# Second product of three batches by seven half-size products instead of one full one

## The chip, the cores and the metric

The kernel runs on one core of a Trainium2 chip. TensorE (PE) multiplies matrices, with its weight loads on a row of their own (PEld); VectorE (DVE), ScalarE (ACT) and GpSimd (POOL) do elementwise work; SyncE (SP) issues most of the transfers. Each engine takes its instructions strictly in the order of the program, and engines wait for one another by semaphores. The metric is the time of one execution in microseconds: the kernel before takes 219.86 us as the median of three runs (219.19 to 220.28).

## The reference

Four batches of 768 rows and 8 heads go through a sparse attention, then through a two-layer network whose hidden width is 2048. Cut to what matters here:

```
# attention, per batch and head: a window of |i-j| < 16 on the keys,
# and 24 block keys (maximum over 32 rows) with 24 block means of v
a = softmax([mask(scale * q @ k.T), scale * q @ k_max.T + log 32])
x = a @ [v, v_mean]                      # 3072 x 512 over all batches
h = x @ w_in                             # first product, 3072 x 2048
g = h * sigmoid(beta * h)
out = g @ w_out                          # second product, 3072 x 512, float32
```

## The kernel before, in words

The work of a batch is attention (scores, exponential, mask, values, normalisation), a transposition of its result into `xT`, the first product into `h_sb` (16 tiles of 128 hidden columns by 768 rows, bf16), and the second product (6 tiles of 128 rows by 512 columns, each a sum over the 16 tiles of `h_sb`).

The order of the instructions is written by hand. `run(main, sides)` (L499) emits the steps of a list `main` one after the other, and after step i every side job whose position lies below i + 1. The main steps keep PE busy, and the side jobs do the attention of the next batch. In the loop over batches 1 to 3 a batch has two stages, which are called the first and the second stage of the batch here:

- First stage: 16 steps `h_tile` (L459), each 8 matmuls of 384 columns into one of three two-bank PSUM tiles `big`, then one ACT pass (Silu) into `h_sb`. Its side jobs prepare the next batch: POOL casts the keys to bf16 (`kq_cast`, L429), SP issues their transposition into `kT` (`kq_dma`, L434), DVE copies the key windows into `kw` and takes block maxima `km` (`windows_nat`, `key_max_nat`), POOL spreads the maxima (`key_sums`), then casts the queries and the values (`kq_cast`, `v_cast`). `v_odd_dma` copies shifted values from `ve` to `vo`.
- Second stage: 24 steps `o_atom` (L482), each 4 matmuls of 512 columns (`o_mm`, L472) into one of two one-bank PSUM tiles `one`. After each sixth of the rows `o_out` (L477) copies the bank to SBUF on DVE and SP issues the output. Its side jobs are the attention of the next batch for four pairs of heads g: `scores` (24 small matmuls into two `big` tiles), the exponential on ACT, the mask on DVE (`mask_e`), the block means (`vm_all`, then `spread` on DVE), the values product `av_at` into a `big` tile, the normalisation on DVE (`norm`: a reciprocal and a multiplication, the result called `xn`), and the transposition of `xn` into `xT`, which is issued from ACT's queue (`x_dma`, L422).

Batch 0 runs by a path of its own, whose second stage also uses `o_atom`, with the attention of batch 1 as side jobs. Batch 3 has no following batch, so its two stages have no side jobs. Its last 128 rows are computed as two halves of 256 columns, so that the last copy and the last output are short.

`natp` and `stage` are pools for casted and loaded keys and queries; a tile of a pool is written again when its last reader is done.

Of the kernel before, what the change touches and what calls it, by code (L numbers as in the profile page):

```python
# [11 lines left out]
def kernel(  # L12
# [10 lines left out]
    nc = tc.nc  # L23
# [48 lines left out]
    stg = {}  # L72
    loads = {}

    krow = const.tile([P, H // 2 * 16 * D], bf16, name="krow")
    qrow = const.tile([P, H // 2 * 16 * D], bf16, name="qrow")
    def row_view(t, b, lo, hi):
        c = CS[b]
        r = S // c
# [107 lines left out]
    h_sb = const.tile([P, k2, S], bf16, name="h_sb")  # L187
    w_in_sb = const.tile([P, k1, d_ff], bf16, name="w_in_sb")
    w_out_sb = const.tile([P, k2, d_model], bf16, name="w_out_sb")
    beta_sb = const.tile([P, k2], f32, name="beta_sb")  # L190
    inv_beta = const.tile([P, k2], f32, name="inv_beta")
    dummy = const.tile([P, 1], f32, name="dummy")
# [234 lines left out]
    nat = {}  # L427

    def kq_cast(eng, nm, b, g):  # L429
        t = natp.tile([P, J6, 2, D], bf16, name=nm + "n", tag=nm + "n")  # L430
        nat[(nm, b, g)] = t
        eng.tensor_copy(out=t[:], in_=stg[(nm, b, g)].rearrange("p h j d -> p j h d"))  # L432

# [16 lines left out]
        nc.scalar.activation(out=h_sb[:, i, lo:lo + HS], in_=t[:, 0:HS], func=ACTF.Silu, scale=beta_sb[:, i:i + 1])  # L450

    def h_part(i, k_lo, k_hi):
        t = big[i % 3]
        for kk in range(2):
            for ki in range(k_lo, k_hi):
                nc.tensor.matmul(t[:, kk, 0:HS], w_in_sb[:, ki, i * P:(i + 1) * P],  # L456
                                 xT[:, ki, kk * HS:(kk + 1) * HS], start=(ki == 0), stop=(ki == k1 - 1))

    def h_tile(i):  # L459
        t = big[i % 3]  # L460
# [16 lines left out]
    def o_out(b, ms, t):  # L477
        o = op.tile([P, d_model], f32, name="o_sb", tag="o_sb")
        (act_cp if b == 0 and ms < 3 else dve_cp)(o[:], t)
        nc.sync.dma_start(out=out_r[b * J6 + ms], in_=o[:])  # L480

    def o_atom(b, ms, a):  # L482
        t = one[ms % 2][:, 0]
        for n in range(4 * a, 4 * a + 4):
            o_mm(ms, n, t)
        if a == 3:
            o_out(b, ms, t)

    def warm(n, t):
        for _ in range(n):  # L490
# [186 lines left out]
    for g in range(G):  # L677
        s.append(((11.2, 14.35, 14.4, 14.5)[g], lambda g=g: x_dma(1, g)))
    s.append((6.5, lambda: load_keys(2)))
    run(main, s)  # L680


    for b in range(1, B):
        n = b + 1
        s = []
        if n < B:
            for g in range(2):
                s.append((0 + .1 * g, lambda g=g, n=n: hw_load("q", q, n, g)))
# [15 lines left out]
        run([lambda i=i: h_tile(i) for i in range(k2)], [x for x in s if x[0] < 16])  # L704
        s = [((x[0] - 16) * 1.2, x[1]) for x in late]
        if n < B:
            scores_at(n, s, [1, 5.9, 8, 10.1])
            av_at(n, s, [10.2, 13.1, 13.2, 13.3], [0, 1, 2, 0])
            for g in range(G):
                s.append(((10.3, 13.35, 13.4, 13.5)[g], lambda g=g: x_dma(n, g)))  # L710
            s.append((5.99, lambda: vm_all(big[0], VMC)))
            s.append((6.3, lambda: spread(0)))
            s.append((8.3, lambda: spread(1)))
            if n + 1 < B:
                s.append((7, lambda n=n: load_keys(n + 1)))
        main = [lambda ms=ms, a=a: o_atom(b, ms, a) for ms in range(J6 - (n == B)) for a in range(4)]
        run(main, s)
        if n == B:
            ms = J6 - 1
            for lo, hi in ((0, 256), (256, 512)):  # L720
                t = one[0 if lo else 1][:, 0]
                for kk in range(k2):
                    o_mm(ms, kk, t, lo, hi)
                o = op.tile([P, hi - lo], f32, name="o_half", tag=f"o_half{lo}", bufs=1)
                nc.vector.tensor_copy(out=o[:], in_=t[:, 0:hi - lo])
                nc.sync.dma_start(out=out_r[b * J6 + ms][:, lo:hi], in_=o[:])

# [1 line left out]
_INS = ['q', 'k', 'v', 'moe_w_in', 'moe_w_out', 'moe_beta']  # L729
# [26 lines left out]
```

## Time and profile before

| | |
|---|---|
| Median of three runs | 219.86 us |
| Span of the profiled execution | 217.3 us, 2.6 us under the median of the runs |
| PE busy | 207.7 us, 96% of the span |
| ACT, DVE, POOL busy | 108.7, 98.7, 55.8 us |
| Granted TensorE clock | full in every slice |

A span runs from the first to the last instruction of the profiled execution; what the runs take beyond it lies around the program. In a row of the timeline stand the start in us, the length in us, engine, line, operation, what is written from what, sizes and count, and in brackets the idle time before and who ended it. A row with a count merges instructions that follow each other. In the groups by line the number after the bar is the busy time in us, then the mean of one instruction in ns.

### The profile page before, as it was taken

The page shows a single profiled execution, that of the slowest core. Times are in us where ns is not written, and L with a number is a line of the kernel's source. Part 1 is how long each engine was busy: PE and PEld are TensorE (multiplying, and loading weights), DVE is VectorE, ACT ScalarE, POOL GpSimd, SP SyncE. Part 2 cuts the span into 40 slices and gives each one's busy share as a digit, 9 for nine tenths or more (in the row PEclk, how much of TensorE's full clock was granted, in tenths as well). Part 3 has the DMA queues.
Part 4 walks back from the last instruction along what each step waited for, and adds up shares of the span by engine and source line. Part 5 has one row for each costly group of instructions (what it writes and reads, how often), then busy time and mean ns, then how long its engine had stood idle before and what let it go on. Part 6 is the DMA issues. An engine that isn't in the chain of part 4 may idle for free.

```text
span 217.3 us, 5298 instructions
## 1 busy us (share of the span) xinstructions
PE 207.7 (96%) x2219; PEld 120.6 (56%) x2219; DVE 98.7 (45%) x232; ACT 108.7 (50%) x144; POOL 55.8 (26%) x89
## 2 busy tenths in 40 slices
PE   7669999999999999999999999999999999999993
PEld 6558766655445455655455456564555556554452
DVE  5378584797476720440589312521797200002121
ACT  2356776787767007666663037767570077750000
POOL 7708991011515600138203300247000000000000
PEclk9999999999999999999999999999999999999999
DMA  6995999999949979999769999999437410001212
GB/s 118 183 217 114 186 180 197 207 207 218 215 100 215 229 220 187 234 202 209 118 183 210 222 250 231 194 191 183 111 111 172 118 51 0 0 0 51 97 48 97
DMA packets 85271, 34.09 MB, mean 157 GB/s; under 512 B 73712, under 2 KB 82304, under 8 KB 85248
## 3 DMA queue, kind: packets, MB, share of 16 engines
q1 hardware_dynamic: 68192, 24.05, 54.4%
q0 software_dynamic: 7424, 7.34, 21.4%
q10 hardware_dynamic: 9632, 2.37, 6.6%
q8 instruction: 17, 0.28, 0.6%
q14 instruction: 6, 0.05, 0.1%
HBM read 27.37 MB, written 6.29 MB: 155 GB/s over the span
## 4 chain that ended last, share of the span: by engine, by line
PE 71%; DMA 14%; DVE 4%; POOL 3%; issue 3%; ACT 2%; SPq 0%; POOLq 0%; ACTq 0%
PE big L456 29%; PE one L474 28%; DMA vst<-in_v_dram 5%; PE big L442 5%; PE one L448 3%; DMA xT<-xn 3%; DMA w_in_sb<-in_moe_w_in_dram 3%; DMA krow<-in_k_dram 3%; PE big L448 2%; PE big L306 1%; POOL ve L324 1%; POOL e L319 1%; PE big L384 1%; DVE e L319 1%; ACT e L315 1%
## 5 line engine op out<-in xcount | busy, mean ns | idle before, releaser
L474 PE MATMUL one<-w_out_sb,h_sb 128*128 128x512 bf16 (+1 forms) x400 | 86.7, 371 | 0.0
L469 ACT ACTIVATE h_sb<-big,beta_sb 128x768 bf16<-128x768 f32 x48 | 42.7, 900 | 52.3 <-PE big L456 52.3
L456 PE MATMUL big<-xT,w_in_sb 128*128 128x384 bf16 x384 | 63.0, 326 | 0.1
L474 PEld LDWEIGHTS <-h_sb 128*128 128x128 bf16 x400 | 37.7, 98 | 40.5 <-issue 0.2
L456 PEld LDWEIGHTS <-w_in_sb 128*128 128x128 bf16 x384 | 37.6, 98 | 25.4 <-issue 0.3
L244 DVE COPY o_sb<-one 128x512 f32<-128x512 f32 x20 | 13.8, 688 | 48.1 <-PE one L474 44.9
L315 ACT ACTIVATE e<-big,bias 128x768 bf16<-128x768 f32 x32 | 27.4, 898 | 8.9 <-PE big L306 4.9
L319 DVE TENSOR_TENSOR e<-e,mask 128x768 bf16<-128x768 bf16 x22 | 13.6, 638 | 20.3 <-ACT e L315 19.4
L238 POOL COPY kw<-km 128x288 bf16<-128x288 bf16 x12 | 5.2, 436 | 50.6 <-DVE km L234 21.0
L324 POOL CAST ve<-vst 128x832 bf16<-128x832 f32 (+1 forms) x15 | 12.9, 875 | 14.1 <-DMA vst<-in_v_dram 12.5
L244 DVE COPY kw<-kT 128x1152 bf16<-128x1152 bf16 x8 | 3.8, 477 | 23.5 <-DMA kT<-kn 23.5
L234 DVE TENSOR_REDUCE km<-kT 128x24 bf16<-128x768 bf16 x12 | 11.2, 944 | 2.6 <-ACT kT L241 2.6
L411 DVE TENSOR_TENSOR xn<-big,r 128x768 bf16<-128x768 f32 x12 | 11.5, 957 | 0.4
L442 PE MATMUL big<-xT,w_in_sb 128*128 128x384 bf16 x64 | 11.4, 327 | 0.1
L432 POOL CAST kn<-kst 128x768 bf16<-128x768 f32 x8 | 6.5, 824 | 15.6 <-DMA kst<-in_k_dram 15.6
L583 ACT ACTIVATE h_sb<-big,beta_sb 128x384 bf16<-128x384 f32 x16 | 8.2, 581 | 3.7 <-PE big L442 3.7
L448 PEld LDWEIGHTS <-w_in_sb 128*128 128x128 bf16 x64 | 6.1, 98 | 4.0
L448 PE MATMUL one<-xT,w_in_sb 128*128 128x384 bf16 x44 | 8.1, 326 | 0.0
L306 PEld LDWEIGHTS <-kw 64*128 64x128 bf16 x288 | 4.9, 95 | 5.5 <-issue 4.2
L442 PEld LDWEIGHTS <-w_in_sb 128*128 128x128 bf16 x64 | 5.8, 98 | 3.7 <-DMA w_in_sb<-in_moe_w_in_dram 0.2
L384 PEld LDWEIGHTS <-e 128*64 128x64 bf16 x336 | 6.1, 111 | 2.3 <-issue 1.9
L450 ACT ACTIVATE h_sb<-one,beta_sb 128x384 bf16<-128x384 f32 x11 | 6.4, 580 | 1.2 <-PE one L448 0.6
(115 smaller groups left out, 191.3 us busy)
## 6 DMA issues: line engine op xcount, KB each, us to landing
out_dram<-o_sb SPq DMA_DIRECT2D x23, 256.0 KB, 2.4
vst<-in_v_dram SPq DMA_DIRECT2D x13, 336.0 KB, 4.6
kst<-in_k_dram SPq DMA_DIRECT2D x8, 384.0 KB, 6.7
qst<-in_q_dram SPq DMA_DIRECT2D x8, 384.0 KB, 4.2
w_in_sb<-in_moe_w_in_dram POOLq DMA_DIRECT2D x4, 512.0 KB, 7.5
w_out_sb<-in_moe_w_out_dram POOLq DMA_DIRECT2D x4, 512.0 KB, 13.7
vo<-ve SPq DMA_DIRECT2D x12, 107.2 KB, 2.3
vst<-in_v_dram SPq DMA_DIRECT2D x3, 416.0 KB, 8.2
```

What stands on the lines that cost most here:

```text
L234: nc.vector.tensor_reduce(out=km[g][:, NK:NK + nb], in_=kT[g][:, W:W + S].rearrange("p (n f) -> p n f", f=block), op=ALU.max, axis=AX.X)
L244: nc.vector.tensor_copy(out=o, in_=i)
L315: nc.scalar.activation(out=e[:], in_=s[:, :, 0:HS], func=ACTF.Exp, bias=bias[:, 0:1], scale=scale)
L319: (nc.gpsimd if (b, g) == (1, G - 1) else nc.vector).tensor_mul(out=e.rearrange("p h (m q) -> p h m q", q=QT), in0=e.rearrange("p h (m q) ...
L324: eng.tensor_copy(out=ve[:, g, lo:hi, 0:D], in_=vst[g][:, lo:hi])
L384: nc.tensor.matmul(tv[par * QT:(par + 1) * QT, j, h], e[:, h, lo:lo + QT], (vo if par else ve)[:, g, h * J6 + J, 0:D + 1], start=True, sto ...
L411: nc.vector.tensor_mul(out=x[:, 3 * us[0]:3 * us[0] + 3 * n].rearrange("p (k j) h d -> p k (j h) d", k=n), in0=tv[:, :, :, 0:D], in1=r[:, ...
L442: nc.tensor.matmul(t[:, 0:HS], w_in_sb[:, ki, i * P:(i + 1) * P], xT[:, ki, 0:HS], start=(ki == 0), stop=(ki == k1 - 1))
L448: nc.tensor.matmul(t[:, 0:HS], w_in_sb[:, ki, i * P:(i + 1) * P], xT[:, ki, lo:lo + HS], start=(ki == 0), stop=(ki == k1 - 1))
L456: nc.tensor.matmul(t[:, kk, 0:HS], w_in_sb[:, ki, i * P:(i + 1) * P], xT[:, ki, kk * HS:(kk + 1) * HS], start=(ki == 0), stop=(ki == k1 - 1))
L469: nc.scalar.activation(out=h_sb[:, i, :].rearrange("p (k m) -> p k m", k=2), in_=t[:, :, 0:HS], func=ACTF.Silu, scale=beta_sb[:, i:i + 1])
L474: nc.tensor.matmul(t[:, 0:hi - lo], h_sb[:, n, ms * P:(ms + 1) * P], w_out_sb[:, n, lo:hi], start=(n == 0), stop=(n == k2 - 1))
```

## The change

The second product of batches 1 to 3 is computed by a Strassen scheme (Winograd's form) on halves. `h_sb` is split in even and odd hidden tiles and in two halves of the rows (A11, A12, A21, A22), `w_out_sb` in even and odd hidden tiles and in two halves of the columns (B11 to B22). Seven products of half size in each direction replace eight. For one 128-row tile of a half (t = 0, 1, 2) a product is 8 matmuls of 256 columns, and it yields 128 rows of the upper and 128 rows of the lower half of the batch.

- `h_sums` forms S1, S2, S4 and S3 in bf16 on DVE, in five pieces per batch among the steps of the first stage (two hidden pairs, two, two, one, one). S3 overwrites A21 in `h_sb`.
- `w_sums` and `w_sums_late` form T1, T2, T4 and T3 once, at the end of batch 0's second stage and after the first step of batch 1's first stage.
- Products 1 and 2, 6 and 7, 5 and 3 share a PSUM bank and add up in it; product 4 has one to itself. The four banks are the two `one` tiles and the two banks of the first `big` tile.
- `gather` takes a partial result out of PSUM after each product: ACT copies after 1, 5 and 2, DVE adds after 6, 7 (two) and 3, POOL adds once after 7. It issues an output of 128 rows after 7 and after 3.
- The attention of the next batch loses the first `big` tile: `av_at` alternates between the other two, `vm_all` still goes to the first. The positions of the side jobs in the second stage are new, counted in 23 steps.
- To make room in SBUF the row-major keys and queries of the first batches share the space of the sums, and pools of keys and queries have fewer buffers. The fourth keys of a batch are loaded at the end of the second stage, into the buffer of the first.

```diff
-    natp = ctx.enter_context(tc.tile_pool(name="nat", bufs=4))
+    half = ctx.enter_context(tc.tile_pool(name="half", bufs=1))
+    natp = ctx.enter_context(tc.tile_pool(name="nat", bufs=2))
...
-        f = stage.tile([P, 2, J6, D], f32, name=nm + "st", tag=nm + "st")
+        f = stage.tile([P, 2, J6, D], f32, name=nm + "st", tag=nm + "st", bufs=3 if nm == "k" else 4)
...
-        t = natp.tile([P, J6, 2, D], bf16, name=nm + "n", tag=nm + "n")
+        t = natp.tile([P, J6, 2, D], bf16, name=nm + "n", tag=nm + "n", bufs=3 if nm == "k" else 2)
...
-        t = big[i % 3]
+        t = big[(i + 2) % 3]
...
+    S1, S2, S4, S3 = s_sb[:, 0], s_sb[:, 1], s_sb[:, 2], A21
+    T1, T2, T4, T3 = t_sb[:, 0], t_sb[:, 1], t_sb[:, 2], B12
+    OPERANDS = {1: (A11, B11), 2: (A12, B21), 3: (S4, B22), 4: (A22, T4), 5: (S1, T1), 6: (S2, T2), 7: (S3, T3)}
+    SLOTS = {1: one[0][:, 0, 0:DH], 6: one[1][:, 0, 0:DH], 4: big[0][:, 0, 0:DH], 5: big[0][:, 1, 0:DH]}
+    SLOTS[2], SLOTS[7], SLOTS[3] = SLOTS[1], SLOTS[6], SLOTS[5]
...
+    def h_sums(lo, hi):
+        j = slice(lo, hi)
+        tt(nc.vector, S1[:, j], A21[:, j], A22[:, j], ALU.add)
+        tt(nc.vector, S2[:, j], S1[:, j], A11[:, j], ALU.subtract)
+        tt(nc.vector, S4[:, j], A12[:, j], S2[:, j], ALU.subtract)
+        tt(nc.vector, S3[:, j], A11[:, j], A21[:, j], ALU.subtract)
...
+    def product(n, t, lo=0, hi=J2):
+        a, b = OPERANDS[n]
+        for j in range(lo, hi):
+            nc.tensor.matmul(SLOTS[n], a[:, j, t * P:(t + 1) * P], b[:, j],
+                             start=(j == 0 and n not in (2, 3, 7)), stop=(j == J2 - 1), skip_group_check=True)
...
+        if n in (1, 5):
+            part[n] = half.tile([P, DH], f32, name=f"p{n}", tag=f"p{n}")
+            act_cp(part[n][:], src)
+        elif n == 6:
+            tt(nc.vector, part[6][:], src, part[1][:], ALU.add)
+        elif n == 2:
+            act_cp(part["lo"][:, 0:DH], src)
+        elif n == 7:
+            tt(nc.vector, u3[:], src, part[1][:], ALU.add)
+            tt(nc.gpsimd, o[:, DH:], part[5][:], u3[:], ALU.add)
+            tt(nc.vector, o[:, 0:DH], SLOTS[4], u3[:], ALU.add)
+        elif n == 3:
+            tt(nc.vector, o[:, DH:], src, part[6][:], ALU.add)
...
+        def first():
+            product(4, 0, 0, J2 - 1)
+        def then():
+            product(1, 0, 0, J2 - 1)
+            product(4, 0, J2 - 1)
+            product(1, 0, J2 - 1)
+            gather(1, b, 0)
+        main = [first, then]
+        for t in range(J6 // 2):
+            for n in ((6, 5, 2, 7, 3) if t == 0 else (1, 6, 5, 4, 2, 7, 3)):
+                main.append(lambda n=n, t=t: step(n, t))
...
-        for g in range(G):
+        for g in range(G - 1):
             hw_load("k", k, n, g)
...
+        for at, lo, hi in ((4.9, 0, 2), (8.9, 2, 4), (12.4, 4, 6), (14.4, 6, 7), (15.9, 7, 8)):
+            s.append((at, lambda lo=lo, hi=hi: h_sums(lo, hi)))
+        run([lambda i=i: h_tile(i) for i in range(k2)], s)
+        s = [(x[0] - 16, x[1]) for x in late]
         if n < B:
-            scores_at(n, s, [1, 5.9, 8, 10.1])
-            av_at(n, s, [10.2, 13.1, 13.2, 13.3], [0, 1, 2, 0])
+            s.append((.05, exp_table))
+            scores_at(n, s, [1, 4.05, 6.05, 8.05])
+            av_at(n, s, [10.1, 11.1, 12.6, 13.7], [1, 2, 1, 2])
             for g in range(G):
-                s.append(((10.3, 13.35, 13.4, 13.5)[g], lambda g=g: x_dma(n, g)))
+                s.append(((10.3, 11.3, 12.8, 13.9)[g], lambda g=g: x_dma(n, g)))
...
+                s.append((20.5, lambda n=n: hw_load("k", k, n + 1, G - 1)))
+        run(second_product(b), s)
```

More of the change, by code (lines that the diff above doesn't have):

```diff
@@ L73 @@
     loads = {}
-    krow = const.tile([P, H // 2 * 16 * D], bf16, name="krow")
-    qrow = const.tile([P, H // 2 * 16 * D], bf16, name="qrow")
+    J2 = d_ff // P // 2
+    DH = d_model // 2
+    s_sb = const.tile([P, 3, J2, HS], bf16, name="s_sb")
+    rows = s_sb.rearrange("p a j s -> p (a j s)")
+    RW = H // 2 * 16 * D
+    krow, qrow = rows[:, 0:RW], rows[:, RW:2 * RW]
     def row_view(t, b, lo, hi):
@@ L189 @@
     w_out_sb = const.tile([P, k2, d_model], bf16, name="w_out_sb")
+    t_sb = const.tile([P, 3, J2, DH], bf16, name="t_sb")
     beta_sb = const.tile([P, k2], f32, name="beta_sb")
@@ L459, in h_tile @@
     def h_tile(i):
-        t = big[i % 3]
+        t = big[(i + 2) % 3]
         if i > 1:
@@ L487, in o_atom @@
             o_out(b, ms, t)
+    hv = h_sb.rearrange("p (j e) s -> p j e s", e=2)
+    wv = w_out_sb.rearrange("p (j e) d -> p j e d", e=2)
+    A11, A12, A21, A22 = [hv[:, :, e, u * HS:(u + 1) * HS] for u in range(2) for e in range(2)]
+    B11, B12, B21, B22 = [wv[:, :, e, u * DH:(u + 1) * DH] for e in range(2) for u in range(2)]
+    S1, S2, S4, S3 = s_sb[:, 0], s_sb[:, 1], s_sb[:, 2], A21
+    T1, T2, T4, T3 = t_sb[:, 0], t_sb[:, 1], t_sb[:, 2], B12
+    OPERANDS = {1: (A11, B11), 2: (A12, B21), 3: (S4, B22), 4: (A22, T4), 5: (S1, T1), 6: (S2, T2), 7: (S3, T3)}
@@ new lines, in w_sums, with w_sums_late @@
+    def w_sums():
+        tt(nc.vector, T1, B12, B11, ALU.subtract)
+        tt(nc.vector, T2, B22, T1, ALU.subtract)
+        tt(nc.vector, T4, B21, T2, ALU.subtract)
+    def w_sums_late():
+        tt(nc.vector, T3, B22, B12, ALU.subtract)
+    def product(n, t, lo=0, hi=J2):
[3 more added lines that the diff above has]
+                             start=(j == 0 and n not in (2, 3, 7)), stop=(j == J2 - 1), skip_group_check=True)
@@ new lines, in second_product, with step @@
+    def second_product(b):
+        def step(n, t):
+            product(n, t)
+            gather(n, b, t)
+        def first():
[9 more added lines that the diff above has]
+                main.append(lambda n=n, t=t: step(n, t))
+        return main
@@ L679 @@
     s.append((6.5, lambda: load_keys(2)))
+    s.append((20, w_sums))
+    s.append((23, lambda: hw_load("k", k, 2, G - 1)))
     run(main, s)
@@ L685 @@
         s = []
+        if b == 1:
+            s.append((.9, w_sums_late))
         if n < B:
```

38 lines of the change are left out of this document (22 added, 16 removed).

## The prediction

> **What bounds the kernel now.** I read the busy times first, then the waits of PE (total, times, longest), then the timeline of PE for the stages; the row at 162.26 is of the chain that ended last.
>
> ```profile
> PE 207.7 (96%) x2219; PEld 120.6 (56%) x2219; DVE 98.7 (45%) x232; ACT 108.7 (50%) x144; POOL 55.8 (26%) x89
> ...
> PE big L257 <- DMA qrow<-in_q_dram: 1.8, 2, 1.4
> ...
> 100.07 1.89 PE L474 MATMUL one<-w_out_sb,h_sb 128*128 128x512 bf16 x8
> ...
> 125.72 2.51 PE L456 MATMUL big<-xT,w_in_sb 128*128 128x384 bf16 x13
> ...
> 146.75 1.89 PE L474 MATMUL one<-w_out_sb,h_sb 128*128 128x512 bf16 x8
> 148.58 0.52 PE L306 MATMUL big<-qn,kw 64*128 64x64 bf16 x24
> 149.03 3.63 PE L474 MATMUL one<-w_out_sb,h_sb 128*128 128x512 bf16 x16
> ...
> 153.05 0.58 PE L358 MATMUL big<-ve,A_avg 128*32 128x128 bf16 x28
> ...
> 162.26 1.26 PE big L384 x72
> ...
> 172.10 20.96 PE L456 MATMUL big<-xT,w_in_sb 128*128 128x384 bf16 x128
> 192.90 20.92 PE L474 MATMUL one<-w_out_sb,h_sb 128*128 128x512 bf16 x112
> ```
>
> PE is busy 96% of the span; its largest wait, 1.8 us in two parts, is on query loads ahead of this loop. Nothing in the loop over batches 1 to 3 makes it wait. The second stages of batches 1, 2 and 3 last 25.65 us (100.07 to 125.72), 25.35 us (146.75 to 172.10) and 20.9 us. So an instruction less on PE is time gained there, as long as the work beside it keeps up.
>
> **What PE gains.** Each batch has 96 matmuls of 512 columns now, and 7 x 8 x 3 = 168 of 256 columns then. The last 128 rows already run 32 such halves:
>
> ```profile
> 193.09:210.00 16.91, 16.91 (x80) 7.69 (x79) 2.77 (x4) 0.90 (x1) 0.00 (x0) 1.00 0.17 63
> ...
> 210.30:213.90 3.60, 3.52 (x33) 2.92 (x30) 1.16 (x3) 0.00 (x0) 0.00 (x0) 1.00 0.30 109
> ```
>
> Second column and count: PE's busy time. A full matmul takes 16.91/80 = 0.211 us (overlap at the edges makes that a little short: batch 3's stage gives 0.217), a half 3.52/33 = 0.107. Their weight loads, 2.92 us of 3.6, still fit behind them. So 168 x 0.107 = 18.0 us, a product of 8 takes 0.86 us, and batch 3 gains 20.8 - 18.0 = 2.8 us on PE. In batches 1 and 2 four times 24 score matmuls (148.58 to 149.03, 0.45 us), the block means (0.6) and four times the values product (1.26/3 = 0.42) are unchanged, 4.1 us: PE alone would need 22.1 us.
>
> **Batch 3.** No other work is on DVE there, its sums are done soon after the last Silu, and the gathers have 1.7 us or more before their bank is written again. The end is dearer: SP has to issue 128 x 512 rows, which wait for an add on POOL, just ahead of the last half.
>
> ```profile
> 213.86 0.42 DVE L725 COPY o_half<-one 128x256 f32<-128x256 f32 x1 [1.32 <-PE one L474]
> ...
> L319 POOL TENSOR_TENSOR e<-e,mask 128x768 bf16<-128x768 bf16 x2 | 3.2, 1634 | 7.3 <-ACT e L315 7.3
> ```
>
> The last copy of 0.42 us becomes an add that I give the same price. POOL's add of 256 columns is at most 1634 x 256/768 = 545 ns, as an estimate. Between nothing and a second output issue with such an add (1.1 us) I take 0.6 us. Batch 3 gains 2.2 us.
>
> **What DVE gets.** Per batch 12 sums of 768 and 8 of 384 bf16 elements in the first stage; in the second stage 12 PSUM operations of 256 columns instead of 6 copies of 512. Rows for prices:
>
> ```profile
> L319 DVE TENSOR_TENSOR e<-e,mask x22: 546/558/1230, 58.8 to 162.1; 128x768 bf16<-128x768 bf16 x22
> ...
> L244 DVE COPY o_sb<-one 128x512 f32<-128x512 f32 x20 | 13.8, 688 | 48.1 <-PE one L474 44.9 <-DMA out_dram<-o_sb 3.2
> L411 DVE TENSOR_TENSOR xn<-big,r 128x768 bf16<-128x768 f32 x12 | 11.5, 957 | 0.4
> L369 DVE COPY vo<-vm_sb 32x768 bf16<-32x768 bf16 x12 | 3.8, 353 | 0.1
> L411 DVE TENSOR_TENSOR xn<-one,r 128x384 bf16<-128x384 f32 x8 | 4.5, 557 | 0.3
> L410 DVE RECIPROCAL r<-big 128x12 f32<-128x12 f32 x12 | 2.7, 226 | 1.9 <-PE big L384 1.8
> L244 DVE CAST vm_sb<-big 32x128 bf16<-32x128 f32 x6 | 1.7, 287 | 1.2 <-ACT vm_sb L241 1.1
> ```
>
> A sum of 768 is the mask's operation: 0.56 us. Halving the length took 957 to 557 ns in the normalisation, so about 0.16 us are fixed, and a sum of 384 costs 0.36. That is 12 x 0.56 + 8 x 0.36 = 9.6 us a batch. The place decides. DVE is in order, and `h_sums(2, 4)` and later stand behind the fourth key maximum:
>
> ```profile
> 96.23 0.94 DVE L234 TENSOR_REDUCE km<-kT 128x24 bf16<-128x768 bf16 x1
> ...
> 143.27 0.95 DVE L234 TENSOR_REDUCE km<-kT 128x24 bf16<-128x768 bf16 x1
> ```
>
> It ends 2.9 and 2.5 us before the second stages of batches 1 and 2. In batch 1 I add 0.7 us: `h_sums(0, 2)` comes ahead of the third window, and T1, T2 and T4 (2048 elements each, an estimate of 1.2 us each by the same slope) delay batch 0's last output copy and, on SP behind it, the key transpositions. From there to the last S2 stand 8 sums of 768 and 6 of 384: 6.65 us. So S2 is complete 4.5 us (batch 1) or 4.1 us (batch 2) into the stage, if nothing disturbs. PE wants its last piece after products 4 and 1 (1.72), the scores (0.45) and seven eighths of product 6 (0.75), at 2.9 us. Here PE begins to wait.
>
> **What disturbs.** At this moment POOL casts queries and values:
>
> ```profile
> 144.37 0.43 POOL L238 COPY kw<-km 128x288 bf16<-128x288 bf16 x1 [3.56 <-PE big L456]
> 144.74 2.37 POOL L432 CAST qn<-qst 128x768 bf16<-128x768 f32 x3
> 147.06 2.53 POOL L324 CAST ve<-vst 128x832 bf16<-128x832 f32 x3
> 151.16 0.88 POOL L324 CAST ve<-vst 128x832 bf16<-128x832 f32 x1 [1.57 <-DMA vst<-in_v_dram]
> ...
> 151.24 1.21 DVE L319 TENSOR_TENSOR e<-e,mask 128x768 bf16<-128x768 bf16 x1 [7.03 <-ACT e L315]
> ...
> 105.34 0.56 DVE L319 TENSOR_TENSOR e<-e,mask 128x768 bf16<-128x768 bf16 x1 [0.23 <-ACT e L315]
> ...
> 105.46 1.18 POOL L324 CAST ve<-vst 128x832 bf16<-128x832 f32 x1 [2.91 <-DMA vst<-in_v_dram]
> ```
>
> At 151.24 a mask multiplication starts 0.08 us into a cast and takes 1.21 instead of 0.56: it ends 0.4 us after the cast. At 105.46 a cast starts inside a multiplication and takes 1.18 instead of 0.88. So an operation with two SBUF inputs on DVE and a cast on POOL run one after the other, and a sum that meets a cast costs 0.65 more. Seven casts and the spreading of the maxima (0.43) fall here. Since the casted queries now have two buffers, the third and fourth cast also wait for the transposition of the first and second. Bounds: no cast meets a sum, or all seven do (0.43 + 7 x 0.65 = 5.0 us). I take the spreading and three casts, those of the second to fourth queries, 2.4 us, because the values' casts stand behind the fourth and so come late. S2 is complete at T = 6.9 and 6.5 us; PE stands some 4 us.
>
> **How long the stage gets.** Behind product 6 on PE wait products 5 and 2 and the scores of the second pair, for these its exponentials, masks, everything. After T, DVE has left: two sums (0.7), 8 masks (4.5), two block-mean copies (0.6), 8 spreads (2.8), 8 gathers of 256 columns (0.42 each, 3.4) and 4 normalisations (1.18 each, 4.7), 16.7 us until the last `xn`. For DVE's own waits in between I take 0.6 us, between nothing and a pair of exponentials (898 ns each, 1.8 us); nearer to nothing, since their order leaves each pair a product or more of lead.
>
> ```profile
> 164.44 3.95 ACTq L423 DMA_TRANSPOSE xT<-xn  x3
> ...
> L315 ACT ACTIVATE e<-big,bias 128x768 bf16<-128x768 f32 x32 | 27.4, 898 | 8.9 <-PE big L306 4.9 <-PE big L298 3.9
> L241 ACT COPY o_sb<-one 128x512 f32<-128x512 f32 x3 | 1.8, 585 | 0.8 <-PE one L474 0.8
> L241 ACT CAST vm_sb<-big 32x128 bf16<-32x128 f32 x6 | 1.5, 256 | 4.0 <-DVE vm_sb L244 4.0
> ```
>
> Now ACT: the issue of a transposition holds its queue 3.95/3 = 1.3 us or more, and the copy of product 1 of the last third stands behind the fourth of them. Before, only Silu stood there, later by a whole stretch of matmuls. Product 2 writes the bank that this copy reads. So after the last `xn` come 1.25 (issue), 0.37 (copy of 256 columns, between 256 and 585 ns), and products 2, 7 and 3, 2.6 us. The stage ends at T + 16.7 + 0.6 + 1.25 + 0.37 + 2.6 = T + 21.5: 28.4 and 28.0 us, instead of 25.65 and 25.35. That is 2.75 + 2.65 = 5.4 us lost.
>
> The fourth keys' late load I put at no cost.
>
> ```profile
> 74.78 0.83 POOL L432 CAST kn<-kst 128x768 bf16<-128x768 f32 x1 [1.05 <-DMA kst<-in_k_dram]
> ...
> 92.05 1.21 SPq L436 DMA_TRANSPOSE kT<-kn  x1
> ```
>
> The fourth cast was over at 75.6, and its transposition was issued only at 92.05, because SP's queue is full of loads and other transpositions. The load now waits on SP for POOL's first key cast, whose buffer it takes, and query loads queue behind it; in batch 2 that cast stands behind POOL's add of the last third, so SP gets on about 1 us into the first stage, where its query loads stood anyway. If this cover goes, the fourth key maximum and with it T move by as much. Two `big` tiles instead of three for the values product are covered by the products between them, T3 by DVE's wait for the first keys.
>
> Sum: 5.4 - 2.2 = 3.2 us more. The profiled span becomes 220.5, and with the 2.6 us by which the median lies above it, 223.1 us.
>
> **Rivals.** (a) No cast gets in the way: T = 4.5 and 4.1, the stages end at 26.0 and 25.6, +0.6 us; with batch 3's gain 219.86 + 0.6 - 2.2 = 218.3. For it: the query transpositions may hold the casts back long enough; against it: the two rows above. (b) The sums get ahead, because they fit in DVE's waits for keys or cost half: PE doesn't wait, T = 2.9, stages of 24.4 us, 219.86 - 1.25 - 0.95 - 2.2 = 215.5. For it speaks the first stage of batch 2, in which DVE was busy 6.11 of 20.7 us:
>
> ```profile
> 126.20:146.90 20.70, 20.63 (x128) 12.42 (x127) 6.11 (x9) 13.33 (x15) 4.58 (x8) 1.00 1.25 210
> ```
>
> Against it speaks the order, which has those sums behind the fourth keys. With PE alone as the bound it would be 211. (c) All casts meet a sum: T = 9.5 and 9.1, 219.86 + 5.35 + 5.25 - 2.2 = 228.3. For it: every dependent pair of sums leaves a gap in which a waiting cast can start. (d) After a stand of 4 us TensorE comes back at a lower clock. At half of it, for as long as it stood, PE would lose 2 us in each of two stages; it needs 22.1 of 28 us and stands 4, so some 2 us are spare and hide about half: 219.86 + 3.2 + 2 = 225.1. The granted clock in the rows above is 1.00, but PE's longest wait in them is 1.4 us, so they neither show nor exclude it. The Trainium skill, "TensorE: Matmul & The Clock Gate", section "Why this matters for your kernels", warns of idle gaps over about 3 us between bursts of matmuls, which one window of idle turns into half speed; no run so far shows it. (e) The halves don't run at half the price in this mix: at 0.124 us each 168 of them take the 20.8 us of before, batch 3 gains nothing and loses 0.6 at its end, 219.86 + 5.4 + 0.6 = 225.9. The row at 210.30 speaks against it.
>
> **How the numbers follow.** The forecast gets 0.48, (a) 0.17, (b) 0.12, (c) 0.13, (d) 0.06, (e) 0.04. A measurement of this kernel can tell about 0.5%, 1.1 us. Faster by more: (b), two thirds of (a) and an edge of the forecast, 0.26; within: the rest of (a) and an edge of the forecast, 0.11; slower 0.63. The forecast's own range is 220 to 226 (two to five casts). The stated range, 215.0 to 228.5, takes in (a), (b) and (c) and leaves PE alone as the bound outside.
>
> **What would show it.** In the changed profile: PE waits for a DVE sum in product 6 early in the second stages of batches 1 and 2, 3 to 5 us each, and none in batch 3; sums of 1.2 us beside POOL casts; a wait of PE for the copy of product 1 on ACT late in the stage; batch 3's second stage at 18 us; granted clock 1.00. I would be wrong if the last S2 is there within 3 us, if the last `xn` comes before 20 us into the stage, or if a second stage of batch 1 or 2 is shorter than 25 us.

## The result and the profile after

The changed kernel takes 250.82 us as the median of six runs (249.33 to 253.38); the kernel before took 219.73 us (219.05 to 222.89) beside it. The ratio is 1.143, with an interval of 1.136 to 1.150. The forecast, 223.1 us, had the direction but a tenth of the size: 3.2 us more were forecast, 31.1 came. From the page of the changed kernel come its span, the busy times and the granted clock in 40 slices (line numbers below are those of the changed kernel: L462 first product, L526 second product, L506 sums and gathers by addition, L247 copies on ACT):

```profile
span 250.9 us, 5808 instructions
...
PE 212.3 (85%) x2414; PEld 144.7 (58%) x2419; DVE 141.1 (56%) x313; ACT 118.0 (47%) x173; POOL 66.9 (27%) x98
...
PEclk9999999999999999959979999985997999999998
```

PE is no longer the bound all the time (85% instead of 96%), and the clock has holes at the places of the second stages of batches 1 and 2. The waits of PE (in total, times, longest) name the cause in the order of size:

```profile
PE one L526 <- DVE s_sb L506: 11.7, 5, 3.4
PE big L526 <- DVE o_sb L506: 10.7, 9, 2.0
PE big L526 <- ACT p L247: 7.3, 6, 2.5
...
PE big L526 <- ACT vm_sb L247: 1.0, 2, 0.5
```

The first row is the wait that was forecast, for the sums. The second and third, 18 us, are waits of products 3 and 4 for gathers, which the prediction had put at nothing. In the fourth, product 5 waits for a copy of the block means, which lie in the other bank of the same `big` tile. The timeline of PE in the second stage of batch 1 shows where they fall (start, length, and in brackets the idle time before):

```profile
100.28 0.93 PE L526 MATMUL big<-t_sb,h_sb 128*128 128x256 bf16 x7
...
104.16 0.39 PE L526 MATMUL one<-t_sb,s_sb 128*128 128x256 bf16 x2 [0.97 <-DVE s_sb L506]
106.48 0.39 PE L526 MATMUL one<-t_sb,s_sb 128*128 128x256 bf16 x1 [1.93 <-DVE s_sb L506]
110.27 0.40 PE L526 MATMUL one<-t_sb,s_sb 128*128 128x256 bf16 x1 [3.40 <-DVE s_sb L506]
110.46 1.91 PE L526 MATMUL big<-t_sb,s_sb 128*128 128x256 bf16 x8
112.17 1.46 PE L526 MATMUL one<-w_out_sb,h_sb 128*128 128x256 bf16 x8
114.02 1.05 PE L526 MATMUL one<-w_out_sb,h_sb 128*128 128x256 bf16 x8
117.09 1.05 PE L526 MATMUL big<-w_out_sb,s_sb 128*128 128x256 bf16 x8 [2.02 <-DVE o_sb L506]
...
125.51 1.03 PE L526 MATMUL big<-t_sb,h_sb 128*128 128x256 bf16 x8 [2.46 <-ACT p L247]
...
141.77 20.96 PE L462 MATMUL big<-xT,w_in_sb 128*128 128x384 bf16 x128
```

The stage lasts 141.77 - 100.28 = 41.5 us instead of 25.65, that of batch 2 40.5 (162.57 to 203.04) instead of 25.35, that of batch 3 23.6 (223.84 to 247.45) instead of 20.9. These are 15.8 + 15.1 + 2.7 = 33.6 us, the whole difference of the spans (250.9 - 217.3); the first stages are unchanged. The stretches of the two long stages, and four pieces of the first of them (PE's busy time is the second number; the clock is the third from the end):

```profile
100.30:141.80 41.50, 27.81 (x390) 20.95 (x389) 26.45 (x52) 13.90 (x24) 9.73 (x12) 0.88 0.61 123
162.60:203.20 40.60, 27.92 (x390) 21.05 (x389) 25.45 (x51) 13.90 (x24) 8.30 (x10) 0.87 0.40 91
...
102.00:106.00 4.00, 1.58 (x32) 0.83 (x30) 3.90 (x7) 2.74 (x5) 1.24 (x2) 1.00 1.00 144
106.00:110.40 4.40, 0.52 (x2) 0.23 (x3) 4.30 (x6) 0.00 (x0) 4.01 (x5) 0.52 0.96 150
110.40:114.00 3.60, 3.60 (x41) 2.52 (x40) 1.75 (x5) 0.70 (x3) 0.00 (x0) 0.63 0.51 119
...
126.00:130.00 4.00, 4.00 (x63) 2.79 (x62) 2.22 (x5) 0.12 (x1) 0.00 (x0) 0.59 0.05 11
```

In 41.5 us PE is idle 13.7 us, and busy 27.8 us with what needs some 22.5 us at full clock: 18.4 for the products, as measured further down with batch 3 alone, and 4.1 for the attention. Three causes lie on top of each other: the late sums (0.97 + 1.93 + 3.40 = 6.3 us idle), the waits of products 3 and 4 (about 7 us idle), and matmuls at a lower clock (5.3 us busy). The clock is low twice, behind the waits for the sums and again from 126.6 us on, behind the wait of 2.46 us.

**A wait without a reason in the data.** Batch 3 shows the second cause undisturbed, since nothing else runs there. Its engines DVE, ACT and PE one after the other:

```profile
229.35 0.42 DVE L506 TENSOR_TENSOR u<-one,p 128x256 f32<-128x256 f32 x1 [2.20 <-PE one L526]
229.87 0.42 DVE L506 TENSOR_TENSOR o_sb<-big,u 128x256 f32<-128x256 f32 x1
```

```profile
234.08 0.37 ACT L247 COPY p<-big 128x256 f32<-128x256 f32 x1 [1.37 <-PE big L526]
```

```profile
230.35 1.03 PE L526 MATMUL big<-w_out_sb,s_sb 128*128 128x256 bf16 x8 [1.10 <-DVE o_sb L506]
...
234.51 1.03 PE L526 MATMUL big<-t_sb,h_sb 128*128 128x256 bf16 x8 [0.50 <-ACT p L247]
```

Product 3 starts 0.06 us after the add of 229.87 is over. This add reads product 4 (`SLOTS[4]`, bank 0 of the first `big` tile), and product 3 accumulates in bank 1. Product 4 starts 0.06 us after the copy of 234.08, which reads product 5, in bank 1, while product 4 writes bank 0. No byte is shared in either case; what is shared is the tile. Three waits of 1.10 and two of 0.50 fall in batch 3. In batches 1 and 2 the same two waits meet late gathers and become 2.02 and 2.46 us.

### The profile page after: what moved, and what is told of

Same layout as the page of the kernel before. It is cut to its first block, busy times and chain, and to the rows that moved or that the text cites. A ratio compares the mean times of both kernels' runs of the same rounds, so it can differ in the third digit from the quotient of the medians.

```text
span 250.9 us, 5808 instructions
## 1 busy us (share of the span) xinstructions
PE 212.3 (85%) x2414; PEld 144.7 (58%) x2419; DVE 141.1 (56%) x313; ACT 118.0 (47%) x173; POOL 66.9 (27%) x98
## 4 chain that ended last, share of the span: by engine, by line
PE 45%; DVE 15%; DMA 15%; SPq 7%; ACT 6%; POOL 5%; issue 5%; ACTq 1%; DVEq 0%; POOLq 0%
PE one L526 9%; PE big L462 8%; PE big L526 8%; DMA kT<-kn 5%; PE one L480 5%; PE big L448 4%; DMA vst<-in_v_dram 4%; DVE s_sb L506 4%; SPq L95 3%; ACT e L321 3%; POOL ve L330 3%; PE one L454 3%; DMA s_sb<-in_k_dram 3%; SPq L442 2%; DVE o_sb L506 2%
## 5 line engine op out<-in xcount | busy, mean ns | idle before, releaser
L462 PE MATMUL big<-xT,w_in_sb 128*128 128x384 bf16 x384 | 62.9, 326 | 0.0
L462 PEld LDWEIGHTS <-w_in_sb 128*128 128x128 bf16 x384 | 37.6, 98 | 24.7
L526 PEld LDWEIGHTS <-s_sb 128*128 128x128 bf16 x216 | 21.0, 101 | 29.6 <-DVE s_sb L506 13.1
L526 PEld LDWEIGHTS <-h_sb 128*128 128x128 bf16 x288 | 28.8, 103 | 13.7 <-issue 8.3
L506 POOL TENSOR_TENSOR o_sb<-p,u 128x256 f32<-128x256 f32 x9 | 6.5, 723 | 100.8 <-DVE u L506 100.8
L526 PE MATMUL one<-w_out_sb,h_sb 128*128 128x256 bf16 x216 | 30.6, 292 | 0.0
L480 PE MATMUL one<-w_out_sb,h_sb 128*128 128x512 bf16 x91 | 21.5, 380 | 0.6 <-issue 0.5
L526 PE MATMUL one<-t_sb,s_sb 128*128 128x256 bf16 x72 | 10.7, 280 | 11.7 <-DVE s_sb L506 11.7
L506 DVE TENSOR_TENSOR u<-one,p 128x256 f32<-128x256 f32 x18 | 7.6, 423 | 22.1 <-PE one L526 18.3
L526 PE MATMUL big<-w_out_sb,s_sb 128*128 128x256 bf16 x72 | 9.3, 272 | 10.7 <-DVE o_sb L506 10.7
L526 PE MATMUL big<-t_sb,h_sb 128*128 128x256 bf16 x72 | 9.8, 272 | 7.3 <-ACT p L247 7.3
L506 DVE TENSOR_TENSOR s_sb<-h_sb 128x768 bf16<-128x768 bf16 (+1 forms) x15 | 8.4, 562 | 13.2 <-ACT h_sb L475 13.2
L247 ACT COPY o_sb<-one 128x256 f32<-128x256 f32 (+1 forms) x12 | 5.1, 426 | 20.1 <-PE one L526 9.3
L247 ACT COPY p<-one 128x256 f32<-128x256 f32 x9 | 3.3, 368 | 20.2 <-PE one L526 14.2
```

The lines of the kernel that those rows point to most:

```text
L247: nc.scalar.copy(out=o, in_=i)
L480: nc.tensor.matmul(t[:, 0:hi - lo], h_sb[:, n, ms * P:(ms + 1) * P], w_out_sb[:, n, lo:hi], start=(n == 0), stop=(n == k2 - 1))
L506: eng.tensor_tensor(out=o, in0=a, in1=b, op=op)
L526: nc.tensor.matmul(SLOTS[n], a[:, j, t * P:(t + 1) * P], b[:, j], start=(j == 0 and n not in (2, 3, 7)), stop=(j == J2 - 1), skip_group_ch ...
```

## The experiments

The first four take one cause away each, or two; the next two price what then remains; the last group has the scheme in batch 3 alone. Lengths are those of the second stages in the profile, from the first matmul of the second product to the first of the next first product.

| Kernel | Batch 1 | Batch 2 | Span |
|---|---|---|---|
| before | 25.65 | 25.35 | 217.3 |
| changed | 41.5 | 40.5 | 250.9 |
| products 4 and 5 in separate tiles | 35.8 | 34.1 | 234.6 |
| no sums of `h_sb` | 34.0 | 34.3 | 236.4 |
| both | 29.5 | 27.7 | 221.7 |
| no value casts beside the sums | 40.6 | 40.4 | 250.1 |

**Separate tiles.** Products 5 and 1 change places: 5 and 3 get the one-bank tile, 4 now has 1 and 2 beside it in the two-bank tile. The block means move to the other tile.

```diff
-    SLOTS = {1: one[0][:, 0, 0:DH], 6: one[1][:, 0, 0:DH], 4: big[0][:, 0, 0:DH], 5: big[0][:, 1, 0:DH]}
+    SLOTS = {1: big[0][:, 1, 0:DH], 6: one[1][:, 0, 0:DH], 4: big[0][:, 0, 0:DH], 5: one[0][:, 0, 0:DH]}
...
-            s.append((7.05, lambda: vm_all(big[0], VMC)))
+            s.append((7.05, lambda: vm_all(one[0], VMC)))
```

> The two halves of the first big tile hold products 4 and 1 (with 2) instead of 4 and 5 (with 3); 5 and 3 go to a one-bank tile, and the block means with them. Theory F (PE waits because the program orders all accesses to a two-bank tile, though product 3 and the add that it waits for use different banks): the waits of product 3 for the DVE add and of product 4 for the ACT copy go. Batch 3's second stage falls from 23.4 us to 18.0 to 18.8, those of batches 1 and 2 by 5 to 8 us each; span 230 to 237 us. Rival S (DVE is simply late in these stages, and another wait takes the place): batch 3 falls as well, but batches 1 and 2 by less than 3 us each; span 240 to 246 us.

It took 236.26 us in one run (219.88 before), its span is 16.3 us shorter than that of the changed kernel, and batch 3 falls from 23.6 to 19.3 us, 0.5 us above the range that was expected. Batches 1 and 2 win 5.7 and 6.4 us, as theory F has it. The waits of PE:

```profile
PE one L526 <- DVE s_sb L506: 11.1, 6, 3.4
PE big L526 <- ACT p L247: 3.7, 2, 1.9
...
PE big L526 <- DVE o_sb L506: 0.5, 2, 0.2
```

The wait for the add went from 10.7 to 0.5 us, that for the copy from 7.3 to 3.7; the wait for the sums is what it was. What is left of the second is the new neighbour: product 4 of the last third waits for the copy of product 1, which product 2, right behind it, needs anyway. So the four banks weren't the four independent places that the prediction took them for.

**No sums.** This kernel leaves out the sums of `h_sb`: products 3, 5, 6 and 7 read A12, A21, A11 and A21 as they are.

```diff
-    OPERANDS = {1: (A11, B11), 2: (A12, B21), 3: (S4, B22), 4: (A22, T4), 5: (S1, T1), 6: (S2, T2), 7: (S3, T3)}
+    OPERANDS = {1: (A11, B11), 2: (A12, B21), 3: (A12, B22), 4: (A22, T4), 5: (A21, T1), 6: (A11, T2), 7: (A21, T3)}
...
-            s.append((at, lambda lo=lo, hi=hi: h_sums(lo, hi)))
+            pass
```

> Leaves out all sums of the first product (S1 to S4 are not formed, their products read quadrants of the first product instead); everything else stays. Theory (sums late by POOL's casts, then a lower clock): the three waits in product 6, 6.3 us in batch 1 and 5.4 in batch 2, go, and with them the part of the lower clock that follows, 2 to 4 us; span 230 to 237 us. Rival F alone (the shared tile rules these stages): the wait moves on to products 3 and 4, and less than 5 us a stage are won; span above 241 us. Batch 3 stays at 23.4 us by both.

It took 238.13 us in one run; the span is 14.5 us shorter, with the tile still shared. The rows for `o_sb` and `p` stay in its waits, 12.2 and 7.3 us, so these waits don't come from the sums.

**Both.** Separate tiles, and the sums of `h_sb` left out.

> Both edits of the two runs before it: other pairs in the two-bank tile, and no sums of the first product (left out). If these two causes hold all of the loss, batches 1 and 2 have second stages of 22 to 26 us, batch 3 18.0 to 18.8, the granted clock is 1.00 throughout, and the span is 208 to 217 us. If there is a third cause (the four transpositions on ACT's queue ahead of the copy of product 1, which the prediction named, or DVE's adds), the stages of batches 1 and 2 stay above 27 us and the span above 220.

It took 223.37 us in one run, span 221.7: 29.2 us less than the changed kernel, where the two alone win 16.3 and 14.5. The two causes add up almost fully, and a third is left, as the second expectation has it. What remains over the kernel before, 4.4 us of span, has these rows among the waits of PE:

```profile
PE big L526 <- ACT p L247: 3.9, 2, 2.1
PE big L526 <- DVE o_sb L506: 2.9, 4, 1.2
```

Even with sums that cost nothing and products 4 and 5 apart, the scheme in all three batches was no gain in this form. The 3.9 us are the copy of product 1 of the last third on ACT; the queue of ACT in the changed kernel shows what it stands behind:

```profile
121.99 1.69 ACT L321 ACTIVATE e<-big,bias 128x768 bf16<-128x768 f32 x2
123.70 1.28 ACT L585 ACT_TABLE_LOAD   x1
...
125.11 0.35 ACT L247 COPY p<-big 128x256 f32<-128x256 f32 x1
...
131.17 5.06 ACTq L429 DMA_TRANSPOSE xT<-xn  x3
136.32 0.37 ACT L247 COPY p<-one 128x256 f32<-128x256 f32 x1 [6.07 <-PE big L526]
```

At 131.17 the issues of three transpositions hold the queue for 5.06 us, and the copy of product 1 comes after them. At 121.99 two exponentials and the load of Silu's table (1.28 us) stand ahead of the copy of product 5, which ends at 125.46; product 4 starts at 125.51, with the 2.46 us above.

**No value casts.** This kernel leaves out the casts of the values of batches 2 and 3 on POOL, which run beside the sums.

```diff
-                s.append((12.6 + 1.2 * g, lambda g=g: v_cast(nc.gpsimd, g)))
```

> The changed kernel without POOL's casts of the values of batches 2 and 3 (left out: the values of batch 1 are used again). Theory (a sum that meets a cast waits for it): the last S2, 9.9 us into the second stage of batch 1 and 8.8 in batch 2, comes 2 to 4 us earlier, and the sums of 384 that took 0.9 to 1.0 us take 0.36. Rival (the sums are slow by themselves or wait for Silu): it stays within 1 us of that.

First the changed kernel, DVE's sums of 384 elements and POOL's casts at the same time:

```profile
105.08 0.35 DVE L506 TENSOR_TENSOR s_sb<-h_sb 128x384 bf16<-128x384 bf16 x1
105.47 0.95 DVE L506 TENSOR_TENSOR s_sb<-s_sb,h_sb 128x384 bf16<-128x384 bf16 x1
106.46 0.91 DVE L506 TENSOR_TENSOR s_sb<-h_sb,s_sb 128x384 bf16<-128x384 bf16 x1
```

```profile
105.39 0.83 POOL L438 CAST qn<-qst 128x768 bf16<-128x768 f32 x1 [2.76 <-DMA qn<-qn]
106.16 3.85 POOL L330 CAST ve<-vst 128x832 bf16<-128x832 f32 x4
```

Then the kernel without the value casts:

```profile
105.73 0.87 DVE L506 TENSOR_TENSOR s_sb<-s_sb,h_sb 128x384 bf16<-128x384 bf16 x1
106.64 0.36 DVE L506 TENSOR_TENSOR s_sb<-h_sb,s_sb 128x384 bf16<-128x384 bf16 x1
```

Alone a sum of 384 takes 0.35 or 0.36 us, beside a cast 0.91 or 0.95. Without the value casts the last piece of product 6 starts 7.5 us into the stage of batch 1 instead of 10.0, and 7.0 instead of 8.9 in batch 2; a query cast still met a sum (0.87). But the span is only 0.8 us shorter (251.84 us in all, one run). The time won in product 6 is lost again behind it: PE's waits for `o_sb` and `p` are 10.2 and 7.3 us, little less than before, and its matmuls run longer at the lower clock. PE is busy 30.1 and 30.0 us in the two stages, where the changed kernel has 27.8 and 27.9, at a mean clock of 0.83 instead of 0.88 and 0.87. So sums that come 2 us earlier were worth little here. That doesn't hold for the sums as a whole: leaving them out won 14.5 us with the same shared tile.

**Transpositions later.** To the separate tiles are added later places for the third and fourth transposition in ACT's queue, behind the copy of product 1. (The positions count the 21 main steps of the second stage, not 23 as said with the change.)

```diff
-                s.append(((10.3, 11.3, 12.8, 13.9)[g], lambda g=g: x_dma(n, g)))
+                s.append(((10.3, 11.3, 14.05, 16.05)[g], lambda g=g: x_dma(n, g)))
```

> The other pairs of the first run (236.3 us), and the third and fourth transposition on ACT's queue are issued after the copies of product 1 and 5 of the last third instead of ahead of both. Theory (ACT's queue holds the copy behind the transpositions, as the prediction says): the wait of product 4 for the ACT copy late in the stage (1.84 and 1.9 us) goes; 1 to 2 us a stage won, span 231 to 233 us. Rival (the transpositions are then late for the next first stage): PE waits there for DMA instead, span 234 to 237 us.

> The kernel with separate banks and later transpositions once more, as the measure for the kernel with the multiplications of a blank tile: 231.4 us by its one run, within 1.5 us.

It took 231.35 us in its one run and 232.11 us (229.28 to 234.29) as the median of six, 1.052 times the kernel before (1.047 to 1.058). The wait for `p` is gone from the list, and the single runs with and without these places differ by 4.9 us, more than the 1 to 2 us a stage that were expected. The rival is out: PE waits for no DMA in the next first stages, which stay at 20.8 us.

**No stand of TensorE.** To the separate tiles, without and with the later transpositions, are added multiplications of a blank tile ahead of the last two pieces of product 6.

```diff
+            if n == 6 and t == 0 and b < B - 1:
+                product(n, t, 0, 6)
+                warm(24, one[0][:, 0, 0:P])
+                product(n, t, 6, 7)
+                warm(48, one[0][:, 0, 0:P])
+                product(n, t, 7)
```

> The other pairs of the first run, and 24 and 48 blank matmuls of 128 columns on PE ahead of the two last pieces of product 6, in batches 1 and 2, while PE waits there for the sums. If the lower clock after that wait costs time: granted clock 1.00 from 106 us on, the two products that follow take 0.87 us each instead of some 1.7, and the span falls by 2 to 4 us to 230 to 233 us. If the stage is bound by DVE and ACT after the last sum anyway: the clock rises as well, but the span stays within 1 us of 234.6.

> Separate banks and later transpositions, and 24 and 48 multiplications of a blank tile ahead of the last two pieces of product 6 in batches 1 and 2, so that TensorE does not stand there. If the slow matmuls after the stand set the end of the stage, some 2.3 us are won in each of the two stages (matmuls of 2.10, 1.92 and 1.54 us become 1.15, 1.04 and 1.03): 4 to 5 us less than the same kernel without them. If DVE's work after the last sum sets it, 0 to 1.5 us less in all.

The first of the two took 238.02 us against 236.26, both in one run each; but it reached the second stage of batch 1 3.0 us later, after a first 25 us at a clock of 0.86 (1.00 in the other), so the two times can't be compared. The second was timed against its own twin: 229.60 us (228.55 to 231.26, six runs) against 232.11, 2.5 us less, though the ranges overlap. The twin, after a wait of 2.79 us:

```profile
108.91 2.10 PE L526 MATMUL one<-t_sb,s_sb 128*128 128x256 bf16 x9 [2.79 <-DVE s_sb L506]
110.80 1.67 PE L526 MATMUL big<-w_out_sb,h_sb 128*128 128x256 bf16 x8
```

And with the blank multiplications in place of the wait:

```profile
110.12 1.15 PE L526 MATMUL one<-t_sb,s_sb 128*128 128x256 bf16 x9
111.10 1.04 PE L526 MATMUL big<-w_out_sb,h_sb 128*128 128x256 bf16 x8
...
113.67 1.03 PE L526 MATMUL one<-w_out_sb,h_sb 128*128 128x256 bf16 x8 [1.07 <-DVE u L506]
```

The matmuls run at full rate, and PE then waits 1.07 us for a gather on DVE. The result, 2.5 us, lies between the two expectations, so the clock sets part of the end of the stages and DVE takes back a part.

How much falls on each stage can be read only after the time of the sums is taken out, since that differs from run to run. The prediction's own division does it: T, from the start of a stage to the end of the last S2, and the rest of the stage behind it. All are single profiles, in us:

| Kernel | T, batches 1 and 2 | Rest, batches 1 and 2 |
|---|---|---|
| forecast | 6.9, 6.5 | 21.5, 21.5 |
| changed | 9.9, 8.9 | 31.6, 31.6 |
| no value casts beside the sums | 7.5, 6.9 | 33.2, 33.5 |
| separate tiles | 10.1, 8.2 | 25.7, 25.9 |
| separate tiles, later transpositions | 10.2, 7.4 | 23.2, 23.4 |
| the same once more (the twin) | 8.7, 7.8 | 22.9, 22.8 |
| the same with blank multiplications | 7.7, 10.5 | 22.6, 21.6 |

Separate tiles take 5.8 and 5.7 us from the rest of the stages, the later transpositions 2.5 to 3.1 more, the blank multiplications 0.3 and 1.2 against the twin. T scatters by up to 3 us among the last four rows, though sums and casts are the same in them. T hangs on the fourth key maximum, behind which the sums stand. In the changed kernel it ends 0.6 us ahead of the stage of batch 1, and the last S2 ends 9.9 us into it:

```profile
98.76 0.94 DVE L240 TENSOR_REDUCE km<-kT 128x24 bf16<-128x768 bf16 x1
...
109.30 0.91 DVE L506 TENSOR_TENSOR s_sb<-s_sb,h_sb 128x384 bf16<-128x384 bf16 x1
```

**Batch 3 alone.** In the kernel before, only batch 3 gets the seven products. Products 4 and 5 have a `big` tile each, the sums of `w_out_sb` run in batch 3's first stage and lie in the space of `kw`, which has no reader left by then; pools, loads and side jobs of batches 1 and 2 are those of before.

```diff
+    t_sb = kw_all.rearrange("p g m k -> p (g m k)").rearrange("p (a j d) -> p a j d", a=3, j=J2)
...
+    SLOTS = {1: one[0][:, 0, 0:DH], 6: one[1][:, 0, 0:DH], 4: big[1][:, 0, 0:DH], 5: big[2][:, 0, 0:DH]}
...
+        if n == B:
+            s = [(1.9, w_sums), (2.9, w_sums_late)]
+            for at, lo, hi in ((4.9, 0, 2), (8.9, 2, 4), (12.4, 4, 6), (14.4, 6, 7), (15.9, 7, 8)):
+                s.append((at, lambda lo=lo, hi=hi: h_sums(lo, hi)))
...
+        run(second_product(b) if n == B else main, s)
```

> The kernel before with the seven products in batch 3 alone, each bank in a PSUM tile of its own (the two one-bank tiles and the first banks of the second and third big tile), the sums of the second matrix in batch 3's first stage. Theory: there the sums meet no cast, no two banks share a tile, so PE waits for nothing: second stage 18.4 us (21 products of 0.87) instead of 20.8, the end 0.6 us later as predicted: 1.5 to 2.2 us faster than before, ratio 0.990 to 0.993. Rival (the gathers or the end cost it): no faster than before.

It took 217.71 us (216.50 to 220.32, ten runs), 0.992 times the kernel before (0.988 to 0.997, 219.49 us beside it): a gain of 1.8 us. The stretch of its last stage:

```profile
192.90:211.30 18.40, 18.40 (x170) 16.33 (x167) 5.71 (x16) 4.25 (x10) 1.56 (x3) 1.00 0.18 65
```

PE is busy without a gap, at full clock. A second version has product 7 ahead of product 2 in the last third, so that the long chain of gathers behind product 7 starts earlier:

```diff
-            for n in ((6, 5, 2, 7, 3) if t == 0 else (1, 6, 5, 4, 2, 7, 3)):
+            for n in ((6, 5, 2, 7, 3) if t == 0 else (1, 6, 5, 4, 2, 7, 3) if t == 1 else (1, 6, 5, 4, 7, 2, 3)):
```

> As the run before, with product 7 ahead of product 2 in the last third, so that its output of 128 rows is issued a product earlier. If SP's issue of that output just ahead of the last one delays the end: 0.3 to 0.8 us less than the run before. If not: the same.

It took 217.82 us, 0.994 (0.991 to 0.997): no gain over the version before that the runs can tell. In the profiles the span ends 3.7 us after the last matmul instead of 4.2, so the order may do what was expected, but the runs of either kernel spread over more than 3 us.

**One tile again.** From the kernel with batch 3 alone, one thing is put back: products 4 and 5 share a tile.

```diff
-    SLOTS = {1: one[0][:, 0, 0:DH], 6: one[1][:, 0, 0:DH], 4: big[1][:, 0, 0:DH], 5: big[2][:, 0, 0:DH]}
+    SLOTS = {1: one[0][:, 0, 0:DH], 6: one[1][:, 0, 0:DH], 4: big[1][:, 0, 0:DH], 5: big[1][:, 1, 0:DH]}
```

> The kernel with the seven products in batch 3 alone and four separate PSUM tiles took 217.7 us, with a second stage of 18.3 us there. Here one thing differs: products 4 and 5 lie in the two banks of one tile. If accesses to the two banks of a tile are ordered as if they were one, product 3 waits three times for an add that reads only the other bank (1.1 us each) and product 4 twice for a copy that reads only the other bank (0.5 us each), 4.3 us, and what they delay: second stage of 22.5 to 23.5 us, time 221.9 to 222.9. If the waits in batch 3 of the changed kernel came from the delays of batches 1 and 2 or from the reading of the bank itself, the stage stays at 18.3 us and the time at 217.7.

It took 221.95 us (221.05 to 223.22), 1.010 times the kernel before (1.006 to 1.013). The shared tile alone costs 4.2 us and turns a gain of 0.8% into a loss of 1%. In the profiles the second stage of batch 3 is 23.5 instead of 18.5 us, and the end behind the last matmul 0.8 us shorter. Its waits of PE:

```profile
PE big L527 <- DVE o_sb L507: 3.2, 3, 1.1
...
PE big L527 <- ACT p L248: 1.0, 2, 0.5
```

They are 4.2 us together, and neither row exists in the kernel with separate tiles. The rival, that the waits came from the delays of batches 1 and 2 or from the reading of the bank itself, is out.

## Why the prediction was right or wrong

- **The step that failed** stands in the part on batch 3: "the gathers have 1.7 us or more before their bank is written again". For the bank that is right; with a tile for each open sum PE doesn't wait once. But the program orders accesses by the tile, and two banks of one tile are one thing to it. Batch 3 lost 2.7 us instead of winning 2.2, and the same waits fell into the stages of batches 1 and 2, where other work delays the gathers. Separating the tiles gave back 16.3 us, half of the 33.6 (one run of each span). "Two `big` tiles instead of three" was argued for the values product only; that products 4 and 5 took their place in the third as neighbours was not priced at all.
- **The length of the stage, T + 21.5, failed with it.** It was a sum over DVE's queue, with PE following behind. The stages of batches 1 and 2 ended at T + 31.6 in the changed kernel, because PE waited for gathers that DVE and ACT reached late: at 116.61 to 117.03 us product 4's add was done only after two masks, and product 3 had to wait for it. With separate tiles and the later transpositions the stages ended at T + 22.8 to 23.4; but the 21.5 had 1.62 us of transposition and copy in them, so what is left is still some 3 us dearer than that sum had it.
- **T itself was mis-sized.** The last S2 was complete at 9.9 and 8.9 us, not 6.9 and 6.5. From the fourth key maximum to it passed 10.5 us in either batch, where 6.65 and 2.4 for POOL were forecast: so POOL cost 3.9 us, more than the spreading and three casts of the forecast and less than the 5.0 of rival (c). The other part is the start: the fourth key maximum ended 0.6 and 1.7 us ahead of the stage instead of 2.2 and 2.5. The prediction had named this as the price if the fourth keys' late load weren't free; no run isolates whether that load did it or the first sums, which stand ahead on DVE. That T came near rival (c)'s 9.5 and 9.1 is thus in part chance. The price of a meeting was right (0.51 to 0.67 more, forecast 0.65), and so was the wait for the sums in product 6 early in the stage. The Trainium skill, "SBUF — State Buffer", section "Who interferes with whom", has a DVE instruction with two SBUF inputs contend with a GpSimd instruction that reads SBUF; the rows of 0.35 and 0.91 us agree. Yet rival (c) would have made 228.3 us: a longer T alone doesn't reach 250.82.
- **The clock, rival (d), was real.** From 106.0 to 110.4 us the granted clock was 0.52 on average, and the next product of 8 took 1.71 us from start to start (110.46 to 112.17) instead of 0.87. The Trainium skill, "TensorE: Matmul & The Clock Gate", section "Why this matters for your kernels", warns of PE standing over about 3 us between bursts, which brings half speed. The trace agrees in the half speed, but not in the length: the clock had fallen before the one wait of more than 3 us began. The forecast gave this rival little weight. Its price of 1 us a stage is near the 1.25 that the medians with separate tiles give (0.3 and 1.2 in the profiles); what the clock took in the changed kernel itself, with several stands in a stage, was not measured alone.
- **Right:** the halves run at half the price (168 in 18.4 us where 18.0 were forecast; rival (e) is out), and batch 3 by itself gains (1.8 us where 2.2 were forecast), with an end that is 0.7 us dearer (4.2 us behind the last matmul, before 3.5) where 0.6 was taken. A copy behind the transpositions on ACT holds up PE late in the stage. There a loss of 1.25 us of issue and 0.37 of copy was forecast in each of two stages, 3.2 us; with separate tiles taking it away was worth 4.2 us (236.26 in one run to 232.11). In the changed kernel itself PE waited there only 0.71 and 0.64 us, in product 4.
- **The direction** was forecast for a cause that held: without the sums the span is 14.5 us shorter. But the signs that the prediction named for being wrong looked only for stages shorter than forecast, and none of them would have caught a stage of 41.5 us.
- **Wrong without weight:** POOL's add of 256 columns took 0.72 us where at most 0.545 was stated; the estimate, scaled from a multiplication of bf16, was too low for this fp32 add:

```profile
L506 POOL TENSOR_TENSOR o_sb<-p,u 128x256 f32<-128x256 f32 x9 | 6.5, 723 | 100.8 <-DVE u L506 100.8
```

What stays open: whether the scheme can win in batches 1 and 2 too, with the sums earlier in DVE's queue and the gathers ahead of the masks. That wasn't tried, nor four one-bank tiles in those stages, where the attention needs the other PSUM tiles; without the sums and with 4 and 5 apart, but the order otherwise unchanged, those stages were still 3.9 and 2.4 us longer than before.

## What to carry to other kernels

When several accumulations share a PSUM tile, ask for each matmul which earlier access of the whole tile it is ordered behind, not which bytes it needs: one tile for each accumulation that lives at the same time, or a wait of a whole gather per product. A scheme that trades PE work for work on DVE, ACT and POOL paid here only in the stage where those stood idle: batch 3 gained and the two busy stages lost in every version that was run. A queue of an engine that also feeds PE must not have slow issues or table loads ahead of what PE waits for.

## What the runs showed of the hardware

In the changed kernel the granted clock was 1.00 up to 106.2 us, when PE had waited 0.97 us, run two matmuls and stood for another 1.65 us; then it was 0.50 until 113.0, and the longest wait, 3.40 us, began only after the fall. In the twin the clock fell 0.86 us into the wait of 1.33 us, after one of 0.95 and two matmuls. In the kernel without value casts it was 0.50 from 105.7 us on, though no wait for the sums was longer than 1.84 us. So no single wait had to be long: a burst of one or two matmuls between two short waits didn't keep the clock up here. It came back only after PE had been busy without a gap again, for 2.8 us in the changed kernel and 4.5 us in the one without value casts.
